# Sign of float64 weights by two integer parts on ScalarE and a second sum on GpSimd, with some softmax normalisations on VectorE

## The chip, the cores and the metric

The kernel runs on one core of a Trainium2 chip. The metric is the device time of that core in microseconds. Before the change it is 1660.12 us (median of three runs, 1659.88 to 1661.93); the execution that was profiled took 1659.89 us, of which 1658.1 us lie between its first and its last instruction. PE is TensorE, DVE is VectorE, ACT is ScalarE, POOL is GpSimd, SP is the engine that issues most DMAs.

## The reference

Attention that keeps only the 32 largest scores of each row, then a two-layer MLP with an exact GELU:

```python
# q, k, v: (8, 8, 576, 64) float32
scores = scale * np.matmul(q, k.transpose(0, 1, 3, 2))
kth = np.partition(scores, -top_k, axis=-1)[..., -top_k:-top_k + 1]   # top_k = 32
scores = np.where(scores >= kth, scores, -1000000000.0)
scores = scores - np.max(scores, axis=-1, keepdims=True)
attn = np.exp(scores)
attn = attn / (np.sum(attn, axis=-1, keepdims=True) + 1e-09)
attn_out = np.matmul(attn, v).astype(np.float32)
# (B, H, S, D) -> (4608, 512)
x = attn_out.transpose(0, 2, 1, 3).reshape(4608, 512)
h = x @ w_in                                   # w_in (512, 2048)
g = 0.5 * h * (1.0 + erf(h * inv_sqrt2))
out = (g @ w_out).astype(np.float32)           # w_out (2048, 512)
```

The two weight matrices arrive as float64, because the product of float64 random numbers with a float stays float64. The matmuls of the kernel are float32, so the kernel turns 2 x 1,048,576 doubles into floats on the chip while the first attention rows are being worked on.

## The kernel before

The program is one loop over slots `n`. A slot handles two tiles of 128 score rows of 576 columns (`e` is 0 or 1), spread over several stages of a pipeline, and up to eight pieces of the MLP. The instruction streams are laid down in this order, and each engine works through its own in order:

```python
    for n in range(ahead):
        left[0] = 7 if START < n < START + 2 * NP else 8     # START = 10, NP = 4: MLP pieces of a slot
        weights_add(unit_in(n))
        scores(n + 2)
        product = attend(n - 3)
        late = n > START
        mlp(1)
        tr = transposes(n - 2)
        # ... (cut)
        softmax(n - 1, 0)
        mlp(1)
        if not late:
            softmax(n - 1, 1)
        # ... transposes, MLP pieces (cut)
        if late:
            softmax(n - 1, 1)
        add_small(n - 1)                # den += 1e-9, on POOL
        # ... more pieces, GELUs (cut)
        top_k(n, {3: lambda: inverse(n - 1)})
        threshold(n)                    # neg, bias: two tiny POOL operations
        normalise(n - 1)

        weights_sign(unit_in(n))
        weights_size(unit_in(n + 1))
        if n >= FIRST:
            load_weights(n + 2)
```

`top_k` is 8 MAX8 and 6 MATCH_REPLACE8 on DVE per slot, with the reciprocal of the row sums of the slot before at its end. `normalise` multiplies the exponentials by that reciprocal, and the transposes of the next slot read them:

```python
    def normalise(i):
        # ... (cut)
        for e in range(2):
            s = row(i, e)                                   # 128 x 576 float32, in place
            nc.gpsimd.tensor_scalar(s, s, st["rden"][:, e : e + 1], None, op0=ALU.mult)
```

The weights come in 16 units of 128 x 1024 numbers, one to a slot: slots 1 to 15, and the last in slot 17. The DMA drops the lowest 16 bits of the first double, so that in the loaded words a 32-bit word holds bits 16 to 47 of a double (`w`) and the next 16 bits hold its sign, its 11 exponent bits and 4 mantissa bits (`first`). The magnitude of the float, read as an integer, is `(first without sign - EXP0) * 2^19 + w * 2^-13`:

```python
    def parts(u):
        t, dst = words[u], weights_of(u)[3]
        return t[:, :, 0::2], t.bitcast(u16)[:, :, 2::4], dst

    def weights_size(u):
        # ... (cut)
        w, first, dst = parts(u)
        size = stage.tile([P, 2 * WS], bf16, tag="size", name="size")
        size = size.rearrange("p (a n) -> p a n", a=first.shape[1])
        nc.scalar.activation(size, first.bitcast(bf16), func=AF.Abs)          # drops the sign bit
        nc.scalar.activation(
            dst.bitcast(i32), size.bitcast(i16), func=AF.Relu, bias=low, scale=2.0**19
        )
        if not on_pool(u):
            nc.scalar.activation(w.bitcast(i32), w.bitcast(u32), func=AF.Copy, scale=2.0**-13)

    def on_pool(u):
        return SLOT_OF[u] >= START                          # slots 10 to 15 and 17

    def weights_add(u):
        if u in words:
            w, _, dst = parts(u)
            d = dst.bitcast(i32)
            if on_pool(u):
                nc.gpsimd.tensor_scalar(
                    w.bitcast(i32), w.bitcast(u32), 2.0**-13, None, op0=ALU.mult
                )
            nc.gpsimd.tensor_tensor(d, d, w.bitcast(i32), op=ALU.add)

    def weights_sign(u):
        if u in words:
            _, first, dst = parts(u)
            top = dst.bitcast(u16)[:, :, 1::2]
            nc.vector.scalar_tensor_tensor(
                out=top, in0=first, scalar=0x8000, in1=top,
                op0=ALU.bitwise_and, op1=ALU.bitwise_or,
            )
        made.add(u)
```

So a unit costs two or three operations on ACT, one or two on POOL, and one on DVE, which copies the sign bit into the finished magnitude.

Of the kernel before, what the change touches and what calls it, by code (L numbers as in the profile page):

```python
# [14 lines left out]
def kernel(  # L15
# [19 lines left out]
    nc = tc.nc  # L35
    f32, i32, u32 = mybir.dt.float32, mybir.dt.int32, mybir.dt.uint32
    bf16, i16, u16 = mybir.dt.bfloat16, mybir.dt.int16, mybir.dt.uint16
    AF = mybir.ActivationFunctionType
    ALU = mybir.AluOpType

    B, H, S, D = q.shape
    P = 128
# [13 lines left out]
    scale = 1.0 / float(D) ** 0.5  # L56
# [3 lines left out]
    const = ctx.enter_context(tc.tile_pool(name="const", bufs=1))  # L60
# [41 lines left out]

    WS = 512
    NWI = KO // 2 * (DFF // WS)
    UNITS = NWI + FT // 2
    EXP0 = 16 * (1023 - 127)
    assert DM == WS and KO == 4 and FT == 16

    def weights_of(u):

        if u < NWI:
            c, r = u // 2 * WS, u % 2 * 2
            return w_in, r, c, w_in_sb[:, r : r + 2, c : c + WS]
        r = 2 * (u - NWI)
        return w_out, r, 0, w_out_sb[:, r : r + 2, :]
# [6 lines left out]
    words = {}  # L124
    low = const.tile([P, 1], f32, name="low")
    nc.gpsimd.memset(low, -EXP0 * 2.0**19)


    SLOT_OF = {u: FIRST + i + (i == UNITS - 1) for i, u in enumerate(ORDER)}
    UNIT_IN = {n: u for u, n in SLOT_OF.items()}  # L130
    unit_in = UNIT_IN.get

    def load_weights(n, queue=None):
# [6 lines left out]
        if src.dtype == f32:  # L140
            for x in range(2):
                queue.dma_start(
                    out=dst[:, x], in_=src[(r + x) * P : (r + x + 1) * P, c : c + WS]
                )
# [7 lines left out]
        else:  # L152
            t = stage.tile([P, 2, 2 * WS], f32, tag="words", name="words")
        for a in range(2):
# [5 lines left out]

    def parts(u):

        t, dst = words[u], weights_of(u)[3]
        return t[:, :, 0::2], t.bitcast(u16)[:, :, 2::4], dst

    def weights_size(u):
        if u not in words:
            return
        w, first, dst = parts(u)
        size = stage.tile([P, 2 * WS], bf16, tag="size", name="size")  # L170
        size = size.rearrange("p (a n) -> p a n", a=first.shape[1])
        nc.scalar.activation(size, first.bitcast(bf16), func=AF.Abs)
        nc.scalar.activation(
            dst.bitcast(i32), size.bitcast(i16), func=AF.Relu, bias=low, scale=2.0**19
        )
        if not on_pool(u):
            nc.scalar.activation(w.bitcast(i32), w.bitcast(u32), func=AF.Copy, scale=2.0**-13)

    def on_pool(u):

        return SLOT_OF[u] >= START

    def weights_add(u):
        if u in words:
            w, _, dst = parts(u)
            d = dst.bitcast(i32)
            if on_pool(u):
                nc.gpsimd.tensor_scalar(
                    w.bitcast(i32), w.bitcast(u32), 2.0**-13, None, op0=ALU.mult
                )  # L190
            nc.gpsimd.tensor_tensor(d, d, w.bitcast(i32), op=ALU.add)

    made = set()

    def weights_sign(u):
        if u in words:
            _, first, dst = parts(u)
            top = dst.bitcast(u16)[:, :, 1::2]
            nc.vector.scalar_tensor_tensor(  # L199
                out=top, in0=first, scalar=0x8000, in1=top,  # L200
                op0=ALU.bitwise_and, op1=ALU.bitwise_or,
            )
        made.add(u)


# [48 lines left out]
    def row(i, e):  # L254
        return S_of[i][:, e * S : (e + 1) * S]
# [97 lines left out]
    def inverse(i):  # L353
        if i < 0 or i >= N:
            return
        st = stat_of[i]
        nc.vector.reciprocal(st["rden"], st["den"])  # L357

    def add_small(i):
        if i < 0 or i >= N:  # L360
            return
        st = stat_of[i]
        nc.gpsimd.tensor_scalar(st["den"], st["den"], 1e-9, None, op0=ALU.add)  # L363

    def softmax(i, e):

        if i < 0 or i >= N:
            return
        st, s = stat_of[i], row(i, e)
        nc.scalar.activation(s, s, func=AF.Prelu, bias=st["neg"][:, e, 1:2], scale=1.0, alpha=STEEP)  # L370
        nc.scalar.activation(  # L371
            s, s, func=AF.Exp, bias=st["bias"][:, e : e + 1], scale=1.0,
            accum_out=st["den"][:, e : e + 1],
        )

    def normalise(i):
        if i < 0 or i >= N:
            return
        st = stat_of[i]
        for e in range(2):  # L380
            s = row(i, e)
            nc.gpsimd.tensor_scalar(s, s, st["rden"][:, e : e + 1], None, op0=ALU.mult)  # L382

    pt_now = [None]
    ptt = const.tile([P, 2, NJ, P], f32, name="ptt")
# [2 lines left out]
    def transposes(i):  # L388

        if i < 0 or i >= N:  # L390
            return []
        t, s = items[i][1], S_of.pop(i)

        def tails():
            tp = ps.tile([P, 512], f32, tag="tp", name="tp_t")
            if t < NM:
                if t % 2 == 0:
                    pt_now[0] = work.tile([P, 2 * NM + 1, 2 * P], f32, tag="pt", name="pt")
                nc.tensor.transpose(tp[:, 0:P], s[:, SM : S + TL], ident)  # L399
                nc.scalar.copy(out=pt_now[0][:, 2 * NM, t % 2 * P : (t % 2 + 1) * P], in_=tp[:, 0:P])  # L400
            else:
                pt_now[0] = ptt
                for r in range(2):
                    nc.tensor.transpose(
                        tp[0:TL, r * P : (r + 1) * P], s[:, r * S + SM : (r + 1) * S], ident
                    )
                for e in range(2):
                    c = slice(e * TL, (e + 1) * TL)
                    nc.scalar.copy(
                        out=halves(ptt[c, 0, NM, :], e, NJ * P), in_=halves(tp[0:TL, 0 : 2 * P], e, P)  # L410
                    )

        def main(e):
            tp = ps.tile([P, 512], f32, tag="tp", name="tp")
            first = e * (S + TL if t < NM else S)
            for j in range(NM):
                nc.tensor.transpose(  # L417
                    tp[:, j * P : (j + 1) * P], s[:, first + j * P : first + (j + 1) * P], ident
                )
            if t < NM:  # L420
                dst = pt_now[0][:, e * NM : (e + 1) * NM, t % 2 * P : (t % 2 + 1) * P]
            else:
                dst = ptt[:, e, 0:NM, :]
            nc.scalar.copy(out=dst, in_=tp.rearrange("p (j n) -> p j n", j=NM))  # L424

        return [tails] + [lambda e=e: main(e) for e in range(2)]
# [137 lines left out]
    def run_gelus():  # L564
        while waiting:
            gelus(waiting.pop(0))
# [9 lines left out]
    def mlp(n):  # L576
        for _ in range(n):
            if done[0] >= len(pieces) or pieces[done[0]][0] > ready[0] or left[0] == 0:
                return
            pieces[done[0]][1]()  # L580
            done[0] += 1
            left[0] -= 1
# [4 lines left out]
    stage = staging.enter_context(tc.tile_pool(name="stage", bufs=1))  # L587
# [26 lines left out]
    first = {2: (0, 1, 1), 3: (2, 2, 3)}  # L614
    prep_in = {}
    for pair in range(2, n_pairs):
        b, p = divmod(pair, NP)
# [3 lines left out]
    for n in range(ahead):  # L621

        left[0] = 7 if START < n < START + 2 * NP else 8
# [6 lines that stand above are left out]
        if product and n > START and done[0] < len(pieces) and pieces[done[0]][0] > ready[0]:  # L630

            for piece in tr[:1]:
                piece()
            tr, ready[0] = tr[1:], n_tok[0]
# [5 lines that stand above are left out]
        prep = prep_in.pop(n, [])  # L640
        if len(prep) > 1 and len(tr) == 3:
            tr, prep = tr[:1] + prep[:1] + tr[1:], prep[1:]
        for piece in tr[:-1]:
            piece()
            ready[0] = n_tok[0]
            mlp(1)
        ready[0] = n_tok[0]
        if late:
            softmax(n - 1, 1)
        add_small(n - 1)  # L650
        for piece in tr[-1:] + prep:
            piece()
            mlp(1)

        run_gelus()
        mlp(left[0])
        run_gelus()
        if n < N:
            top_k(n, {3: lambda: inverse(n - 1)})
        else:  # L660
            inverse(n - 1)
        threshold(n)
        normalise(n - 1)

        weights_sign(unit_in(n))
        weights_size(unit_in(n + 1))
        if n >= FIRST:
            load_weights(n + 2)
        if n <= NP:
            load("v", n)  # L670
# [38 lines left out]
```

## Time and profile before

| | before |
|---|---|
| time, median of 3 | 1660.12 us |
| PE busy | 1590.1 us (96%) |
| DVE busy | 1428.5 us (86%) |
| ACT busy | 1182.8 us (71%) |
| POOL busy | 661.6 us (40%) |
| the sign on DVE (line 199) | 16 operations, 1291 to 1379 ns, first at 31.6 us, last at 213.5 us |
| one normalisation on POOL (line 382) | 288 operations, median 1722 ns |

The page of a profile gives the busy time of each engine over the whole span and its share in 40 slices of 41.45 us. A view of stages gives the busy time of each engine between two moments. A timeline lists instructions in order with start and duration; "x2" merges two of a kind, and a bracket tells how long the engine had stood idle and what released it. Neighbouring DVE or ACT instructions overlap by some 0.1 us in these lists, so the cost of one in a full row is the distance from its start to the start of the next, not its duration.

### The profile page before, as it was taken

What the parts mean: (1) busy time and instruction counts of PE and PEld (TensorE: products, weight loads), DVE (VectorE), ACT (ScalarE), POOL (GpSimd) and SP (SyncE); (2) the same over time, 40 slices, a digit from 0 to 9 for tenths busy, and PEclk for the clock granted to TensorE, in tenths of its full rate; (3) what the DMA queues carried; (4) which work ended last, traced back from release to release, by engine and by line L of the source; (5) the groups of instructions that cost most, each with busy time, mean ns of one, the idle gap of its engine ahead of it and who ended that gap; (6) DMA issues with size and microseconds to landing.
All of it is one profiled execution on the core that took longest, in us unless ns stands there. A gap on an engine that the chain in (4) does not pass through costs nothing.

```text
span 1658.1 us, 25071 instructions
## 1 busy us (share of the span) xinstructions
PE 1590.1 (96%) x8832; PEld 1079.1 (65%) x8832; DVE 1428.5 (86%) x3043; ACT 1182.8 (71%) x2131; POOL 661.6 (40%) x761
## 2 busy tenths in 40 slices
PE   6559999999999999999999999999999999999999
PEld 4336566766666667676666667676666666666665
DVE  7999899998999898998999888998889898999800
ACT  6888777777777777777777777777777777777720
POOL 3769653333333333333333333333333333333300
PEclk7779999999999999999999999999999999999999
DMA  6422210011100111001110111001110001000000
GB/s 162 138 99 97 84 49 1 14 29 29 37 14 22 29 30 35 1 28 36 29 28 1 43 29 43 1 14 28 44 35 1 27 15 32 5 14 3 5 13 13
DMA packets 126621, 56.14 MB, mean 34 GB/s; under 512 B 117760, under 2 KB 117792, under 8 KB 126496
## 3 DMA queue, kind: packets, MB, share of 16 engines
q1 hardware_dynamic: 125376, 54.25, 12.2%
q8 instruction: 70, 1.15, 0.3%
q14 instruction: 55, 0.45, 0.1%
q10 hardware_dynamic: 1056, 0.26, 0.1%
q0 software_dynamic: 64, 0.03, 0.0%
HBM read 45.08 MB, written 9.44 MB: 33 GB/s over the span
## 4 chain that ended last, share of the span: by engine, by line
PE 89%; DVE 6%; ACT 2%; POOL 1%; issue 1%; POOLq 0%; ACTq 0%
PE h_ps L500 30%; PE y_ps L536 29%; PE o L448 8%; PE s_ps L284 7%; PE tp L417 7%; DVE top L331 3%; DVE rest L334 3%; PE tp_qk L239 2%; PE t_ps L280 2%; PE o L459 1%; PE tp_t L399 1%; PE s_ps L305 1%; POOL s L382 1%; DVE w_in_sb L199 0%; ACT s L371 0%
## 5 line engine op out<-in xcount | busy, mean ns | idle before, releaser
L331 DVE MAX8 top<-rest 128x8 f32<-128x576 f32 x864 | 609.9, 748 | 0.0
L500 PE MATMUL h_ps<-xT,w_in_sb 128*128 128x256 f32 (+1 forms) x2560 | 554.5, 361 | 3.7 <-ACT g L511 3.7
L536 PE MATMUL y_ps<-w_out_sb,g 128*128 128x512 f32 x1152 | 549.4, 599 | 0.0
L382 POOL TENSOR_SCALAR s<-s,rden 128x576 f32<-128x576 f32 x288 | 493.5, 1723 | 1.0 <-issue 0.7
L500 PEld LDWEIGHTS h_ps<-xT,w_in_sb 128*128 128x128 f32 x2560 | 429.2, 191 | 66.7 <-issue 16.8
L334 DVE MATCH_REPLACE8 rest<-top,rest 128x576 f32<-128x576 f32 x576 | 423.7, 744 | 0.0
L363 POOL TENSOR_SCALAR den<-den 128x2 f32<-128x2 f32 x144 | 32.0, 222 | 831.7 <-ACT s L371 830.7
L536 PEld LDWEIGHTS y_ps<-w_out_sb,g 128*128 128x128 f32 x1152 | 195.0, 190 | 166.4 <-issue 164.3
L288 ACT ACTIVATE s<-s_ps 128x1024 f32<-128x1024 f32 x128 | 131.5, 1027 | 166.5 <-PE s_ps L284 144.8
L371 ACT ACTIVATE s<-s,bias 128x576 f32<-128x576 f32 x288 | 223.3, 775 | 13.0 <-ACT s L370 0.4
L370 ACT ACTIVATE s<-s,neg 128x576 f32<-128x576 f32 x288 | 224.0, 778 | 0.5 <-POOL neg L346 0.4
L424 ACT COPY pt<-tp 128x512 f32<-128x512 f32 x256 | 147.1, 575 | 103.6 <-PE tp L417 103.4
L334 DVE MATCH_REPLACE8 rest<-top,s 128x576 f32<-128x576 f32 x288 | 211.9, 744 | 0.0
L417 PEld LDWEIGHTS tp<-ident,s 128*128 128x128 f32 x1152 | 147.9, 145 | 89.3 <-issue 59.2
L331 DVE MAX8 top<-s 128x8 f32<-128x576 f32 x288 | 201.9, 743 | 3.9 <-ACT s L289 3.9
L417 PE MATMUL tp<-ident,s 128*128 128x128 f32 x1152 | 177.9, 279 | 4.3 <-ACT pt L400 4.2
L448 PE MATMUL o<-pt,raw_v 128*64 128x256 f32 x1280 | 155.1, 389 | 0.0
L284 PE MATMUL s_ps<-qk 64*128 64x256 f32 x1024 | 151.8, 417 | 0.7 <-ACT s L288 0.7
L357 DVE RECIPROCAL rden<-den 128x2 f32<-128x2 f32 x144 | 23.2, 161 | 139.9 <-POOL den L363 139.3
L448 PEld LDWEIGHTS o<-pt,raw_v 128*64 128x64 f32 x1280 | 87.5, 139 | 65.8 <-issue 23.9
L284 PEld LDWEIGHTS s_ps<-qk 64*128 64x128 f32 x1024 | 91.8, 194 | 23.7 <-issue 1.8
L511 ACT ACTIVATE g<-h_ps 128x512 f32<-128x512 f32 x144 | 78.6, 595 | 34.0 <-PE h_ps L500 33.2
(63 smaller groups left out, 1070.2 us busy)
## 6 DMA issues: line engine op xcount, KB each, us to landing
raw_q<-in_q_dram SPq DMA_DIRECT2D x64, 128.0 KB, 2.3
raw_v<-in_v_dram SPq DMA_DIRECT2D x64, 128.0 KB, 2.4
out_dram<-y SPq DMA_DIRECT2D x32, 256.0 KB, 2.1
w_out_sb<-in_moe_w_in_dram SPq DMA_DIRECT2D x16, 511.8 KB, 4.8
raw_k<-in_k_dram SPq DMA_DIRECT2D x62, 128.0 KB, 2.4
w_out_sb<-in_moe_w_out_dram SPq DMA_DIRECT2D x10, 511.8 KB, 3.9
words<-in_moe_w_out_dram SPq DMA_DIRECT2D x6, 511.8 KB, 4.7
raw_q<-in_q_dram SPq DMA_DIRECT2D x64, 16.0 KB, 2.2
```

Of the source, the lines that this page charges most:

```text
L284: nc.tensor.matmul(s_ps[:, e, c * 256 : (c + 1) * 256], lhsT=lhsT[rows, :], rhs=qk[rows, KT + c * 256 : KT + (c + 1) * 256], start=True, s ...
L288: nc.scalar.activation(spread(s, S + TL, SM), s_ps, func=AF.Copy, scale=scale)
L331: nc.vector.max(st["top"][:, e, 8 * r : 8 * r + 8], cur[e])
L334: nc.vector.match_replace(rest[:, e], st["top"][:, e, 8 * r : 8 * r + 8], cur[e], LOWEST)
L370: nc.scalar.activation(s, s, func=AF.Prelu, bias=st["neg"][:, e, 1:2], scale=1.0, alpha=STEEP)
L371: nc.scalar.activation(s, s, func=AF.Exp, bias=st["bias"][:, e : e + 1], scale=1.0, accum_out=st["den"][:, e : e + 1],)
L382: nc.gpsimd.tensor_scalar(s, s, st["rden"][:, e : e + 1], None, op0=ALU.mult)
L417: nc.tensor.transpose(tp[:, j * P : (j + 1) * P], s[:, first + j * P : first + (j + 1) * P], ident)
L424: nc.scalar.copy(out=dst, in_=tp.rearrange("p (j n) -> p j n", j=NM))
L448: nc.tensor.matmul(o[e * D : (e + 1) * D, 0:n], lhsT=vt[:, j, e, :], rhs=pt[:, e * NM + j if j < NM else 2 * NM, :], start=(j == 0), stop= ...
L500: nc.tensor.matmul(h_tile(u)[:, i, :], lhsT=w_in_sb[:, ko, f * P : (f + 1) * P], rhs=xT[:, ko, c0 : c0 + n], start=(ko == 0), stop=(ko == ...
L536: nc.tensor.matmul(y_of[sub], lhsT=g_of[u][:, i, sub * P : (sub + 1) * P], rhs=w_out_sb[:, f, :], start=(f == 0), stop=(f == FT - 1),)
```

## The change

The sign no longer comes from DVE. ACT makes two whole-number parts from `first` read as a signed 16-bit number: a Relu gives the part of positive numbers and zero for negative ones, as before; a Prelu gives the part of negative numbers, sign bit and all, and a number that rounds to zero for positive ones (scale 2^-21 and slope 2^40 below zero together give 2^19). The second part overwrites the word that held `first`. POOL adds both parts and `w`. The step that took the absolute value is gone, so ACT still has two such operations per unit; POOL has one sum more, and DVE none. To relieve POOL, the normalisation of the slot is moved to DVE: one of the two tiles where the next slot has a unit whose multiplication is done on ACT, both where that multiplication is on POOL too. All other slots keep both on POOL.

```diff
+    high = const.tile([P, 1], f32, name="high")
+    nc.gpsimd.memset(high, EXP0 * 2.0**-21)
...
     def parts(u):
-        t, dst = words[u], weights_of(u)[3]
-        return t[:, :, 0::2], t.bitcast(u16)[:, :, 2::4], dst
+        t, dst = words[u], weights_of(u)[3].bitcast(i32)
+        return t[:, :, 0::2], t.bitcast(mybir.dt.int16)[:, :, 2::4], t[:, :, 1::2].bitcast(i32), dst
...
-        w, first, dst = parts(u)
-        size = stage.tile([P, 2 * WS], bf16, tag="size", name="size")
-        size = size.rearrange("p (a n) -> p a n", a=first.shape[1])
-        nc.scalar.activation(size, first.bitcast(bf16), func=AF.Abs)
-        nc.scalar.activation(
-            dst.bitcast(i32), size.bitcast(i16), func=AF.Relu, bias=low, scale=2.0**19
-        )
+        w, first, below, d = parts(u)
+        nc.scalar.activation(d, first, func=AF.Relu, bias=low, scale=2.0**19)
+
+        nc.scalar.activation(below, first, func=AF.Prelu, bias=high, scale=2.0**-21, alpha=2.0**40)
...
     def weights_add(u):
         if u in words:
-            w, _, dst = parts(u)
-            d = dst.bitcast(i32)
+            w, _, below, d = parts(u)
             if on_pool(u):
                 nc.gpsimd.tensor_scalar(
                     w.bitcast(i32), w.bitcast(u32), 2.0**-13, None, op0=ALU.mult
                 )
+            nc.gpsimd.tensor_tensor(d, d, below, op=ALU.add)
             nc.gpsimd.tensor_tensor(d, d, w.bitcast(i32), op=ALU.add)
-
-    def weights_sign(u):
-        # ... (the whole function, as above)
...
-    def normalise(i):
+    def normalise(i, on_dve):
...
-            nc.gpsimd.tensor_scalar(s, s, st["rden"][:, e : e + 1], None, op0=ALU.mult)
+            (nc.vector if e >= 2 - on_dve else nc.gpsimd).tensor_scalar(
+                s, s, st["rden"][:, e : e + 1], None, op0=ALU.mult
+            )
...
-        normalise(n - 1)
-
-        weights_sign(unit_in(n))
+        u = unit_in(n + 1)
+
+        normalise(n - 1, 0 if u not in words else 2 if on_pool(u) else 1)
+
         weights_size(unit_in(n + 1))
```

## The prediction

> **What bounds the kernel now.** I read the page first (engines over the 40 slices), then the kernel in stages, then the timelines of DVE, POOL and ACT in one slot, then the waits.
>
> The 40 slices:
>
> ```profile
> PE   6559999999999999999999999999999999999999
> DVE  7999899998999898998999888998889898999800
> POOL 3769653333333333333333333333333333333300
> ```
>
> The first four slices differ from the rest: PE half idle, DVE full, POOL at its busiest. All weight units are made there (first sign at 31.6 us, last at 213.5). The stages (columns: stretch, its length, then busy time of each engine, granted clock, DMA):
>
> ```profile
> 12.00:32.85 20.85, 11.72 (x58) 7.46 (x58) 20.66 (x43) 16.68 (x27) 4.24 (x5) 0.74 0.63 164
> 32.85:119.98 87.13, 47.47 (x236) 32.34 (x238) 87.13 (x176) 72.60 (x121) 59.48 (x49) 0.68 0.38 117
> 119.98:224.74 104.76, 93.42 (x517) 62.53 (x514) 96.88 (x198) 82.03 (x141) 80.53 (x60) 0.98 0.28 84
> 224.74:1440.00 1215.26, 1215.26 (x6958) 828.41 (x6958) 1100.15 (x2363) 896.03 (x1640) 457.71 (x564) 1.00 0.10 25
> ```
>
> In 32.85 to 119.98 us (slots 2 to 9) DVE is busy for all 87.13 us: it alone sets the pace, 10.9 us a slot, and PE waits at half load. From 119.98 to 224.74 us (slots 10 to 18) the MLP has begun and nothing is full: DVE 96.9, PE 93.4, ACT 82.0, POOL 80.5 of 104.8 us. After that PE has no gap for 1215 us. So whatever the first 225 us lose or gain goes straight to the end, and nothing after them can be changed by this edit, which keeps PE's program as it is.
>
> The end of slot 4 on DVE, and POOL beside it:
>
> ```profile
> 62.88 1.42 DVE L331 MAX8 top<-rest 128x8 f32<-128x576 f32 x2
> 64.20 0.15 DVE L357 RECIPROCAL rden<-den 128x2 f32<-128x2 f32 x1
> 64.27 1.30 DVE L199 SCALAR_TENSOR_TENSOR w_in_sb<-w_out_sb,w_in_sb 128x1024 uint16<-128x1024 uint16 x1
> 65.45 1.42 DVE L331 MAX8 top<-s 128x8 f32<-128x576 f32 x2
> ...
> 64.38 1.25 POOL L346 TENSOR_SCALAR neg<-top 128x4 f32<-128x4 f32 x1 [2.86 <-DVE rden L357]
> 65.71 0.19 POOL L349 TENSOR_TENSOR bias<-neg 128x2 f32<-128x2 f32 x1
> 65.89 3.43 POOL L382 TENSOR_SCALAR s<-s,rden 128x576 f32<-128x576 f32 x2
> 69.28 2.40 POOL L191 TENSOR_TENSOR w_out_sb<-w_out_sb 128x1024 int32<-128x1024 int32 x1
> 71.77 0.22 POOL L363 TENSOR_SCALAR den<-den 128x2 f32<-128x2 f32 x1
> ```
>
> The reader is to see three things. The sign costs DVE 65.45 - 64.27 = 1.18 us from start to start (1.22 in other slots). POOL's tiny neg takes 1.25 us here, as long as the sign lasts; at 129.80 us, where it does not start behind a sign, it takes 0.23. And POOL has time: 2.86 us idle before neg.
>
> Who waits in the stage from 120 us:
>
> ```profile
> PE tp_t L404 <- POOL s L382: 2.9, 2, 1.5
> PE tp_t L399 <- POOL s L382: 2.8, 3, 1.7
> PE h_ps L500 <- ACT g L511: 2.6, 1, 2.6
> DVE rden L357 <- POOL den L363: 7.6, 5, 4.3
> ```
>
> 5.7 us of PE's idle time there end with POOL's normalisation. DVE's 7.6 us end with den, which in turn waits for ACT's exponentials (21.0 us in the same view): those are PE's and ACT's lateness, not POOL's.
>
> **What the Trainium skill says.** "VectorE: DVE Perf Modes", section "Mode 2×_2P — use both read ports for one tensor": a float32 tensor_scalar from SBUF to SBUF makes two elements a cycle. Section "The TRN2 errata — SBUF-src ops pay a fixed extra latency per instruction" gives 58 cycles plus the elements by the mode, at 0.96 GHz. The trace agrees for one element a cycle: MAX8 of 576 would be 634 cycles, 0.66 us, and two of them take 1.32 from start to start (62.88 to 64.20). No run shows the two-element mode yet. "SBUF — State Buffer", section "Who interferes with whom": a DVE operation with two SBUF inputs or in a two-port mode and a GpSimd operation hold a shared port in turn. The neg of 1.25 against 0.23 us agrees. "ScalarE: Activation LUTs", section "What ACT_TABLE_LOAD costs": the cost does not depend on the function. The trace agrees: Relu 1.15, Abs 1.14, Copy 1.13 us for 1024 elements.
>
> **The change part by part.**
>
> *DVE, slots 1 to 9.* Removed: 9 signs x 1.21 = 10.9 us, all on the path. Added: an estimate for a normalisation of 576 elements at two a cycle is (58 + 288) / 0.96 = 0.36 us. It needs the reciprocal just before it, so it must wait for that one's end: 0.15 - 0.07 us of it remain, and some 0.05 for the signal; I take 0.15. Slots 1 to 8 get one normalisation (8 x 0.51 = 4.1), slot 9 two (0.87): 5.0 us. Port: neg wants to start at the same moment as the normalisation; one of them waits for the other. If it is DVE half the time, 9 x 0.5 x 0.2 = 0.9 us. Sum: -10.9 + 5.0 + 0.9 = -5.0 us.
>
> *ACT.* Abs and Relu (62.58 to 64.81 us, 2.23) become Relu and Prelu, 2 x 1.05 start to start without a wait between: -0.1 us per unit. No table load is added: Prelu already runs in this kernel on either side of a GELU without one. ACT has about 9.2 us of work per early slot (72.6 us in eight slots), below the 10.3 us that a slot is to take. No gain, no new bound.
>
> *POOL, slots 1 to 9.* Plus 2.40 for the second sum, minus 1.72 for one normalisation, and neg is held up for 0.4 instead of 1.2. About the same load, 7.4 of 10.3 us; it stays off the path.
>
> *POOL, slots 10 to 17.* The row there now: multiplication 2.99, sum 2.41, normalisations 3.42, neg, bias and den 1.5 to 1.7, about 10.0 us of a slot. After: 2.99 + 4.8 + 0.9, 8.7 us. So it is relieved.
>
> *DVE in slots 10 to 17.* Seven signs x 1.22 = 8.5 us go, six pairs of normalisations x 0.87 = 5.2 come (slots 10 to 14 and 16): 96.9 falls to 93.6 us.
>
> *PE in the same stage.* Three waits for POOL's normalisation (1.66, 0.58 and 0.52 us) follow slots in which both tiles move to DVE, where they end some 1 us after the reciprocal and not 4.6. They should vanish: -2.8 us. The two before the transposes of slot 18 (1.54 and 1.41) stay on POOL, but bias there takes 1.11 us behind a sign and should take 0.19: -0.9 us. With DVE's shorter row that is about -4 us; the wait for the GELU (2.57) and the table loads stay.
>
> Sum: -5 - 4 = -9, so 1660 becomes 1651.
>
> **The rivals.**
>
> *A: DVE takes the gain back.* The normalisation does not reach two elements a cycle, or waits for a whole POOL operation. At one element a cycle it is 0.66 us: 9 slots cost 0.3 more each, 10 x 0.3 = 3 us of the first stage, and 3.6 in the second. If it waited 1.7 us for POOL's own normalisation each time, the slot would be longer than before, 8 x 0.5 to 1 us. Against the latter: in POOL's order neg, bias and its own normalisation come after the same reciprocal, so DVE should be first. A would make 1655 to 1664.
>
> *B: POOL's longer chain becomes the bound in slots 10 to 15.* Both sums now follow ACT's two parts, and den, which comes after them in POOL's order, frees the reciprocal. In slot 11 ACT ends its part at 135.2 us, so POOL would end at 135.2 + 2.99 + 4.8 = 143.0 if the multiplication too had to wait for ACT (they touch the same tile), 140.0 if not; den ran at 141.57. That is up to 1.5 us in each of two or three slots. For it: den already stood within 0.1 us of the reciprocal in slot 10. Against it: three of POOL's 10 us are gone. B would take back 2 to 4 us: 1653 to 1655.
>
> *C: slots 10 to 18 were DVE's more than I think.* Then the whole slack of 104.8 - 93.6 us opens up, or most of it: another -4, 1646 to 1647. Against it: DVE waits 7.6 us there itself.
>
> **Range and chances.** The middle is 1651.5, a little above the sum for B. The range takes A in its mild form at one end and most of C at the other: 1645.5 to 1657.5. 2% is 33 us; the stage in which anything can happen is 225 us long and its removable part under 25, so faster by 2% has 0.01, slower by 2% 0.01.
>
> **What the profile after would show.** The first step is right if DVE is still full in slots 2 to 9 and a slot takes 10.1 to 10.5 us, with a normalisation of about 0.45 us in the list; it is wrong if such a normalisation lasts 0.7 us or more. The waits of the transposes (line 399) for a normalisation should vanish around slots 10 to 15. B shows as DVE's reciprocal waiting for den with POOL's sums right before it. The stage of 1215 us should have the same length. The prediction fails if ACT sets the pace of the early slots, or if an early slot is longer than 10.9 us.

## The result, and the profile after

| | before | after |
|---|---|---|
| time, median of 6 | 1660.12 us | 1655.54 us (1654.10 to 1656.98) |
| ratio | | 0.9967, 95% interval 0.9954 to 0.998 |
| profiled span | 1658.1 us | 1653.7 us |

The change makes the kernel 0.3% faster: 4.6 us by these medians, inside the predicted range, but only half of the predicted 8.6. The size of the gain depends on which runs are compared: all 44 runs of the kernel before in this study have a median of 1661.9 us, the ten of the changed kernel 1655.4, which makes 6.5 us, and the trace of before is of one of its shorter runs (1659.89 us). The 40 slices of the kernel after:

```profile
PE   6669999999999999999999999999999999999999
DVE  7999899989999889998989988998889898999800
POOL 3677543333333333333333333333333333333300
```

On DVE the slices hardly differ; POOL's fullest slice has gone from 9 to 7. The stages of the kernel after, cut at the same slots as before (stretch, length, busy PE, weight loads, DVE, ACT, POOL, clock, DMA):

```profile
33.62:115.89 82.27, 50.54 (x234) 32.23 (x236) 81.70 (x178) 73.05 (x121) 57.63 (x49) 0.62 0.42 132
115.89:220.49 104.60, 93.24 (x518) 62.67 (x517) 93.93 (x203) 83.47 (x143) 69.25 (x51) 0.98 0.25 76
220.49:1435.75 1215.26, 1215.26 (x6958) 828.86 (x6958) 1100.02 (x2362) 896.13 (x1640) 457.52 (x563) 1.00 0.10 25
```

Slots 2 to 9 went from 87.13 to 82.27 us, with DVE still full. Slots 10 to 18 went from 104.76 to 104.60, although POOL lost 11 us of work there and DVE 3. In the long stage PE is busy without a gap, as before; that it takes as long as before is read from the last column of the table below, since the stretch here was cut to the length of the one before.

The same end of slot 4 on DVE, and POOL beside it, in the kernel after:

```profile
63.19 0.14 DVE L349 RECIPROCAL rden<-den 128x2 f32<-128x2 f32 x1
63.36 0.52 DVE L375 TENSOR_SCALAR s<-s,rden 128x576 f32<-128x576 f32 x1
63.81 1.41 DVE L323 MAX8 top<-s 128x8 f32<-128x576 f32 x2
...
63.35 0.23 POOL L338 TENSOR_SCALAR neg<-top 128x4 f32<-128x4 f32 x1 [2.58 <-DVE rden L349]
63.66 0.28 POOL L341 TENSOR_TENSOR bias<-neg 128x2 f32<-128x2 f32 x1
63.92 1.73 POOL L375 TENSOR_SCALAR s<-s,rden 128x576 f32<-128x576 f32 x1
65.62 2.40 POOL L193 TENSOR_TENSOR w_out_sb<-w_out_sb 128x1024 int32<-128x1024 int32 x1
68.10 2.40 POOL L194 TENSOR_TENSOR w_out_sb<-w_out_sb 128x1024 int32<-128x1024 int32 x1
70.58 0.22 POOL L355 TENSOR_SCALAR den<-den 128x2 f32<-128x2 f32 x1
```

One normalisation costs DVE 63.81 - 63.36 = 0.45 us, and 0.17 from the reciprocal's start to its own. Neg is back at 0.23 us, only bias shows a trace of the shared port (0.28 against 0.19).

Who kept PE waiting in slots 10 to 18 of the kernel after, and DVE in the same stretch. The "tails" are the last 64 columns of both tiles of a slot, which PE transposes first (`tp_t`) and ACT copies to `pt`; `tp` are the transposes of the other columns, `h_ps` is the first MLP product, `g` its GELU:

```profile
PE tp L412 <- ACT pt L395: 3.8, 3, 1.5
PE tp_t L399 <- POOL s L375: 3.0, 2, 1.6
PE h_ps L495 <- ACT g L506: 2.7, 1, 2.7
...
DVE rden L349 <- POOL den L355: 10.0, 6, 4.0
```

The same wait for the copy of the tails in the kernel before:

```profile
PE tp L417 <- ACT pt L400: 2.0, 2, 1.3
```

The waits of line 399 of before, which should vanish (2.8 us), are gone: that line is 394 here, and no wait of it is left. Line 399 here is line 404 of before, the two transposes of slot 18, whose 2.9 us are now 3.0. In place of the vanished waits PE waits longer for ACT's copy of the tails (3.8 us, it was 2.0) and 0.6 us for another of ACT's copies, and DVE waits 10.0 us for den and not 7.6. Most of the time was moved, not saved.

For the experiments below, one measure is used throughout: the distances between the reciprocals on DVE, which stand at the end of every slot. The table gives them for one trace of each kernel (two where it says so), in us; the last column is from the end of slot 18 to the end of the kernel.

| kernel | slots 2 to 9 | slot 10 | slots 11 to 17 | slot 18 | rest |
|---|---|---|---|---|---|
| before | 87.23 | 11.03 | 83.68 | 11.23 | 1433.5 |
| after | 82.37 | 10.77 | 84.24 | 10.43 | 1433.5 |
| after, a second trace | 82.38 | 10.78 | 86.24 | 10.44 | 1433.5 |
| normalisations alone moved | 91.91 | 12.90 | 90.98 | 12.41 | 1434.9 |
| conversion alone | 78.67 | 12.42 | 90.47 | 10.62 | 1434.8 |
| one of two late ones on DVE | 82.38 | 10.93 | 83.42 | 10.31 | 1433.5 |
| early ones on POOL | 78.64 | 12.48 | 87.09 | 10.70 | 1434.8 |
| no Prelu in late units | 82.37 | 10.77 | 80.10 | 10.43 | 1433.5 |
| no second sum | 82.38 | 10.77 | 86.06 | 10.42 | 1433.5 |
| tails first, two traces | 82.37, 82.39 | 10.78, 10.77 | 81.22, 83.50 | 10.43, 10.43 | 1433.5, 1433.5 |
| PE kept busy | 92.56 | 10.93 | 87.94 | 10.46 | 1435.1 |
| PE kept busy, tails first | 93.38 | 10.96 | 85.47 | 10.43 | 1433.5 |
| the same, early ones on POOL | 92.55 | 10.95 | 85.48 | 10.43 | 1433.5 |

### The profile page after: what moved, and what is told of

Its sections match the earlier page's. It is cut to its first block, busy times and chain, and to the rows that moved or that the text cites. A ratio compares the mean times of both kernels' runs of the same rounds, so it can differ in the third digit from the quotient of the medians.

```text
span 1653.7 us, 25056 instructions
## 1 busy us (share of the span) xinstructions
PE 1593.8 (96%) x8832; PEld 1080.5 (65%) x8832; DVE 1419.6 (86%) x3049; ACT 1184.1 (72%) x2131; POOL 650.5 (39%) x756
## 3 DMA queue, kind: packets, MB, share of 16 engines
q1 hardware_dynamic: 125376, 54.25, 12.2%
q8 instruction: 70, 1.15, 0.3%
## 4 chain that ended last, share of the span: by engine, by line
PE 92%; ACT 6%; DVE 1%; issue 1%; POOL 0%; ACTq 0%; POOLq 0%; DVEq 0%
PE h_ps L495 30%; PE y_ps L531 30%; PE o L443 9%; PE s_ps L276 8%; PE tp L412 8%; PE tp_qk L231 2%; PE t_ps L272 2%; ACT s L363 1%; PE o L454 1%; ACT s L362 1%; PE s_ps L297 1%; PE tp_t L394 1%; ACT s L280 1%; POOL s L375 0%; PE warm L595 0%
## 5 line engine op out<-in xcount | busy, mean ns | idle before, releaser
L375 POOL TENSOR_SCALAR s<-s,rden 128x576 f32<-128x576 f32 x266 | 456.0, 1723 | 0.8 <-issue 0.4
```

What stands on the lines that cost most here:

```text
L375: (nc.vector if e >= 2 - on_dve else nc.gpsimd).tensor_scalar(s, s, st["rden"][:, e : e + 1], None, op0=ALU.mult)
```

## The experiments

The theory after the first traces: slots 2 to 9 are DVE's row and gave what was predicted; slots 10 to 18 are set by PE and ACT in their fixed orders, so an earlier normalisation only waits elsewhere. Rivals: POOL's second sum took the gain back there (rival B), or the second tile's move was worth something that another loss hides.

**The changed kernel again.** No edit.

> The changed kernel once more, beside the others of this group. 1654 to 1657 us. If the 0.9 us by which its first row of scores came later in the first trace belongs to the change, it is there again; if it is the warm-up matmuls' clock, the start differs from run to run in kernels whose start is the same.

1654.93 us (1654.37 to 1656.68), ratio 0.9961 (0.9946 to 0.9975). Its first scores came 0.1 us later than in the kernel before, and not 0.9: the 16 warm-up matmuls ahead of them (32 entries of the trace) lasted 5.77 us in the trace of before, 6.67 in the first of after and 5.87 here. So 0.9 us of the first trace is chance, and not the change's. The gain of slots 2 to 9 is the same to 0.01 us; slots 11 to 17 differ by 2 us between the two traces.

**The normalisations alone.** The conversion of before, with the new line in the slot:

```diff
-        normalise(n - 1)
+        u = unit_in(n + 1)
+        normalise(n - 1, 0 if u not in words else 2 if on_pool(u) else 1)
```

> The old conversion with the sign on DVE, and only the normalisations moved. If the first stage is DVE's row alone, a slot there takes 10.9 + 0.6 = 11.5 us, eight of them 5 us more than before. If moved normalisations bring nothing in slots 10 to 18 (theory: PE and ACT in their fixed order set the pace there), the whole is 1664 to 1667 us. If they are worth the 3 to 4 us of PE's waits for them that I predicted (rival), it is 1660 to 1663.

1676.26 us, ratio 1.0088 (1.0073 to 1.0103): some 10 us above the theory's guess and more above the rival's. Slots 2 to 9 are as expected (8 x 11.5 = 92). Slots 10 to 14 take 12.9 us each, and DVE is full in them: its search for the 32 largest (9.7 us, as in the early slots of the run below with every normalisation on POOL), 1.1 for the reciprocal and both normalisations, and 2.1 for the sign from start to start. DVE and POOL at the end of slot 12 of this kernel show why the sign takes so long:

```profile
162.46 0.95 DVE L382 TENSOR_SCALAR s<-s,rden 128x576 f32<-128x576 f32 x2
163.32 2.27 DVE L199 SCALAR_TENSOR_TENSOR w_in_sb<-w_out_sb,w_in_sb 128x1024 uint16<-128x1024 uint16 x1
...
162.68 0.35 POOL L349 TENSOR_TENSOR bias<-neg 128x2 f32<-128x2 f32 x1
163.11 3.12 POOL L188 TENSOR_SCALAR words<-words 128x1024 int32<-128x1024 uint32 x1
```

POOL, free of its normalisations, starts its multiplication 0.2 us ahead of the sign, and the sign takes 2.27 us where it took 1.32; so it is in six slots (2.19 to 2.31 us). Before, the sign always started first, and it was POOL's neg or bias that was lengthened. "SBUF — State Buffer" of the Trainium skill, section "Who interferes with whom", says just that: issue order decides who blocks. Here the later one did not wait for the whole of the earlier one (3.12 us) but lost 0.95. That is 6 us of the some 10. The theory had also left out that DVE's row alone is longer in these slots: 9.7 + 1.1 + 1.2 = 12.0 us even with an undisturbed sign, where slot 10 of before took 11.0. So the two halves of the change do not add up: one is 14 us slower alone, and the pair is faster than the kernel before.

**The conversion alone.**

```diff
-        normalise(n - 1, 0 if u not in words else 2 if on_pool(u) else 1)
+        normalise(n - 1, 0)
```

> The new conversion, and every normalisation on POOL as before. If DVE alone set the pace of the first stage, a slot there would fall to 9.7 us, 4 us less than in the changed kernel, and the whole would be 1651. But POOL then has 3.4 + 4.8 + 1.2 us a slot, and ACT 9.4 to 10.2: with them as the next bound (theory) a slot stays at 10.1 to 10.4. In slots 10 to 15 POOL has 12.3 us a slot (3.0 + 4.8 + 3.4 + 1.1) and must become the bound: 5 to 8 us lost there. Theory: 1660 to 1664 us.

1660.73 us, ratio 0.9995 (0.9986 to 1.0004): no difference from before, as the theory had it. Slots 2 to 9 take 78.67 us, 3.7 less than with one normalisation on DVE; that is faster than expected of POOL and ACT. In slots 12 to 14 POOL is the bound (in slot 11 it waits 2.3 us for ACT's second part besides). Its row in slot 12, with 12.3 us from den (138.19) to den, and DVE's wait between 108 and 225 us:

```profile
138.98 3.43 POOL L375 TENSOR_SCALAR s<-s,rden 128x576 f32<-128x576 f32 x2
142.50 2.99 POOL L190 TENSOR_SCALAR w_out_sb<-w_out_sb 128x1024 int32<-128x1024 uint32 x1
145.57 2.40 POOL L193 TENSOR_TENSOR w_in_sb<-w_in_sb,w_out_sb 128x1024 int32<-128x1024 int32 x1
148.05 2.40 POOL L194 TENSOR_TENSOR w_in_sb<-w_in_sb,w_out_sb 128x1024 int32<-128x1024 int32 x1
150.53 0.22 POOL L355 TENSOR_SCALAR den<-den 128x2 f32<-128x2 f32 x1
...
DVE rden L349 <- POOL den L355: 25.3, 9, 5.9
```

So relieving POOL in the late units is needed, to pay for the second sum. It is no gain by itself, as the run before this one shows.

**One of two late normalisations back on POOL.**

```diff
-        normalise(n - 1, 0 if u not in words else 2 if on_pool(u) else 1)
+        normalise(n - 1, 0 if u not in words else 1)
```

> In slots 9 to 14 and 16 only one of the two normalisations is on DVE, the other on POOL. POOL's row in those slots is 3.0 + 4.8 + 1.7 + 0.9 = 10.4 us of some 11.6. Theory (PE and ACT set the pace there, moved normalisations bring nothing by themselves): within 1 us of the changed kernel, 1654 to 1657. Rival (the normalisation's lateness costs what I predicted): 1.5 to 2 us slower or more.

1655.10 us, ratio 0.9961 (0.9946 to 0.9975), the same as the changed kernel beside it. The second tile's move brings nothing; the rival falls.

**Both early normalisations back on POOL.**

```diff
-        normalise(n - 1, 0 if u not in words else 2 if on_pool(u) else 1)
+        normalise(n - 1, 0 if u not in words else 2 if on_pool(u) else 0)
```

> Slots 1 to 8 keep both normalisations on POOL (as in the run with all of them on POOL, whose slots there took 9.7 to 9.9 us against 10.3), slots 9 to 14 and 16 have both on DVE (as in the changed kernel). If the two stages add up (theory: the first is DVE's row, and POOL's 9.6 us a slot fits just beside it), 3.7 us less than the changed kernel: 1651 to 1652. Rival: ACT, which had 10.2 us of every 10.3 in slots 5 to 9, comes late into slot 10 and gives the gain back there: 1653 to 1655.

1656.28 us, ratio 0.9968 (0.9956 to 0.998): nothing won. DVE is 3.7 us ahead at the end of slot 9 and has lost it by the end of slot 11 (12.48 us for slot 10, 15.72 for slot 11). ACT's part of the unit of slot 10, in the changed kernel and then in this one:

```profile
112.13 1.24 ACT L174 ACTIVATE w_out_sb<-w_out_sb,low 128x1024 int32<-128x1024 int16 x1
```

```profile
112.15 1.24 ACT L174 ACTIVATE w_out_sb<-w_out_sb,low 128x1024 int32<-128x1024 int16 x1
```

In both it stands at the same time: ACT did not follow DVE's gain. From slot 5 on these operations stand 9.9 us apart in this kernel (62.85 to 112.15 us), of which ACT works 9.1 and waits the rest for PE; the 10.2 of the expectation is too high, in the changed kernel ACT works 9.0 us a slot there. ACT begins its next unit 6.67 us after the reciprocal of slot 10 here and 2.98 us after it in the first trace of the changed kernel, and slot 11 is longer by the same 3.7 us. So the mechanism of the rival is the right one, though the median lies a little above the rival's range.

**Less work on ACT in the late units.** This kernel leaves out the negative part of the seven units of slots 10 to 15 and 17; POOL adds w twice.

```diff
-        nc.scalar.activation(below, first, func=AF.Prelu, ...)
+        if not on_pool(u):
+            nc.scalar.activation(below, first, func=AF.Prelu, ...)
...
-            nc.gpsimd.tensor_tensor(d, d, below, op=ALU.add)
+            nc.gpsimd.tensor_tensor(d, d, w.bitcast(i32) if on_pool(u) else below, op=ALU.add)
```

> Leaves out the second part (Prelu) of the seven units of slots 10 to 15 and 17; POOL adds w a second time in its place, so its row stays. Negative weights of these units come out as nonsense. ACT loses 7 x 1.15 = 8 us between 112 and 201 us. If ACT's fixed order sets the pace of slots 10 to 18 together with PE (theory): 2 to 4 us faster than the changed kernel, 1651 to 1653. If it is PE's row alone or DVE's: no change, 1654 to 1656.

1651.79 us, ratio 0.9946 (0.993 to 0.9963): 3 to 4 us below the changed kernel by the medians, with intervals that overlap (0.9954 to 0.998 and 0.9946 to 0.9975 there). Its trace is of its shortest run (1650.67 us). Slots 11 to 17 take 80.1 us in it, 4 to 6 less than in the two traces of the changed kernel; without slot 11, in which two traces of one kernel differ by 2 us, slots 12 to 17 take 69.3 us against 72.2 and 72.0. So of the 8 us taken from ACT somewhat less than half comes through. PE's longest waits between 114 and 220 us there:

```profile
PE tp_t L400 <- POOL s L376: 3.0, 2, 1.6
PE h_ps L496 <- ACT g L507: 2.7, 1, 2.7
PE tp L413 <- ACT pt L396: 2.5, 2, 1.4
```

The wait for the copy of the tails falls from 3.8 to 2.5 us.

**Less work on POOL.** This kernel leaves out the sum of the second part in all units.

```diff
-            nc.gpsimd.tensor_tensor(d, d, below, op=ALU.add)
```

> Leaves out POOL's sum of the second part in all 16 units (negative weights come out without their magnitude and sign part), ACT unchanged. POOL loses 2.4 us a slot. Theory (POOL is beside the path in all slots): 1654 to 1656. Rival B of the prediction (the chain from ACT's parts over two sums to den holds up DVE): 2 to 4 us faster.

1655.96 us, ratio 0.9967 (0.9954 to 0.998): the same as the changed kernel, though 38 us of POOL's work (16 x 2.4) are gone. Rival B falls.

**The tails ahead of the softmax.** If ACT's order is what holds PE's transposes, moving the copy forward must help. In the branches in front of the first softmax half, for slots 10 to 18:

```diff
+        elif START <= n <= START + 2 * NP:
+            for piece in tr[:1]:
+                piece()
+            tr = tr[1:]
         softmax(n - 1, 0)
```

> In slots 10 to 18 the transpose of the tails and its copy on ACT stand ahead of the first softmax half, not behind it, since the normalised rows are now there earlier. Theory: PE's waits for that copy (3.8 us in slots 10 to 18 of the changed kernel) go, and 2 to 3 us of the whole, 1652 to 1653. Rival: the softmax, and den behind it, only come later by as much, and nothing is won: 1654 to 1656.

1654.36 us (1651.77 to 1654.71), ratio 0.9953 (0.9938 to 0.9968): a median in the rival's range. Once more:

> The kernel with the tails ahead of the softmax in slots 10 to 18 once more, in more rounds. Its first trace had slot 10 to slot 18 in 91.7 us (94.7 and 96.7 in two traces of the changed kernel), but its median was only 0.6 to 1.2 us below the changed kernel's. Theory: 1 to 3 us faster than the changed kernel's 1655, 1652 to 1654. Rival: no difference, 1654 to 1656.

1652.85 us (1652.03 to 1654.02), ratio 0.9947 (0.9935 to 0.996). PE's longest waits between 114 and 220 us in the second trace:

```profile
PE h_ps L495 <- ACT g L506: 3.4, 1, 3.4
PE tp_qk L231 <- ACT pt L419: 2.8, 4, 1.0
PE tp_t L399 <- POOL s L375: 1.6, 2, 1.4
```

The wait for the tails' copy has gone from the list. Slots 13 to 15 take 10.8 to 10.9 us each, where the changed kernel has 11.7, 12.2 and 14.9; slot 16 then takes 15.8, where it has 11.8, so the long slot is mostly put off by one. In the table slots 11 to 17 are 0.7 to 5 us shorter, by which traces are compared; slots 12 to 17 alone take 69.9 us in both traces, 2.1 to 2.3 less than in the two of the changed kernel. This is the fastest complete kernel of the study: its nine runs have a median of 1653.4 us, 2.0 below the ten of the changed one. The two intervals of the ratios (0.9935 to 0.996 and 0.9954 to 0.998) touch, so the size of that gain is not certain.

**PE kept busy in slots 2 to 9.** The traces of one kernel differed by 2 us in slot 11, and PE's granted clock reached its full value at different times. Two stretches of the first and second trace of the changed kernel (the clock is the third number from the end):

```profile
116.00:118.00 2.00, 2.00 (x18) 1.15 (x15) 2.00 (x6) 0.20 (x2) 2.00 (x1) 0.94 0.32 131
```

```profile
116.00:118.00 2.00, 2.00 (x12) 1.21 (x12) 2.00 (x6) 1.19 (x2) 1.96 (x1) 0.51 0.00 0
```

Slot 11 took 12.0 us in the first and 14.3 in the second. In the two traces with the tails first it took 11.3 and 13.6, with 1.00 and 0.50 as the clock of this stretch. To see whether the clock is the cause, 24 and 12 matmuls of the identity were put where PE waits:

```diff
+        t = ps.tile([P, 512], f32, tag="l1", name="warm")
+        for _ in range(count):          # 24 ahead of the transposes, 12 before the last of them
+            nc.tensor.matmul(t[:, 0:P], lhsT=ident, rhs=ident, start=True, stop=True)
```

> The changed kernel with 36 matmuls of the identity in each of slots 2 to 9, in two places where PE waits; their result is not used. In the changed kernel PE's clock is at half there, and full only from 115 to 119 us on, so that slot 10's products take 3.1 to 3.4 us and not 2.3, and the copies of ACT wait for slow transposes. Theory (that clock is part of what made slot 10 late and two traces of one kernel differ): slot 10 starts PE at full clock, 1 to 2 us gained, 1653 to 1654, and a narrower range of runs. Rival: the added matmuls hold up PE's own row in the early slots, and ACT behind it, 1656 or more.

> Both of the former together. If the two gains are apart: 1651 to 1653. If the clock is not the cause: as the tails alone.

> Both of the former, and the normalisations of slots 1 to 8 on POOL. With these on POOL alone DVE came to the end of slot 9 3.6 us earlier, but ACT's part of slot 9 ended at the same time as in the changed kernel (112.15 against 112.13 us) and nothing was won. Theory (ACT's row sets the pace from slot 5 on): ACT's work is the same here, only its waits for PE are shorter (2.7 us between 81 and 112 us); at most 2 us below the one with the former two, 1650 to 1652. If POOL's row (9.6 us a slot) holds it up: as the former two or slower.

The theories of all three missed, and the rival of the first was right: 1669.56, 1666.51 and 1666.62 us, ratios 1.0045 (1.0031 to 1.0059), 1.0026 (1.0016 to 1.0037) and 1.0028 (1.0017 to 1.004). PE in one early slot of the first:

```profile
70.39 5.62 PE L620 MATMUL warm<-ident 128*128 128x128 f32 x48
75.86 0.27 PE L394 MATMUL tp_t<-ident,s 128*128 128x128 f32 x1
75.96 0.60 PE L412 MATMUL tp<-ident,s 128*128 128x128 f32 x4
76.40 2.84 PE L620 MATMUL warm<-ident 128*128 128x128 f32 x24
79.08 0.60 PE L412 MATMUL tp<-ident,s 128*128 128x128 f32 x4
```

A float32 matmul of the program is two entries of the trace, so the added work was 8.4 us a slot and not half of it: it filled PE and held up ACT behind it (slots 2 to 9: 92.6 us). The clock was full there, but the run cannot tell what that was worth.

The traces lead further back, to slot 4. PE's product with v there (20 matmuls), in the first and the second trace of the changed kernel:

```profile
54.14 2.68 PE L443 MATMUL o<-pt,raw_v 128*64 128x256 f32 x20
53.34 3.94 PE L443 MATMUL o<-pt,raw_v 128*64 128x256 f32 x20
```

The clock between 52 and 56 us was 0.65 in the first and 0.50 in the second. ACT waits 1.07 and 2.33 us for this product and does not make the loss good in the slots that follow, in which it works some 9 of every 10.3 us. It begins its next unit 2.98 and 5.24 us after the reciprocal of slot 10, and slot 11 takes 12.02 and 14.28 us: both differ by 2.26. Seven traces of the changed kernel and its late variants agree: where this product took 2.7 to 2.9 us slot 11 took 10.8 to 12.0, where it took 3.9 to 4.2 slot 11 took 13.6 to 14.3. So slot 11 shows ACT's lateness, which begins with a slow product at a low clock seven slots earlier. This is read from traces; no run changed that clock alone.

## Why the prediction was right in range, and which half of it failed

- **DVE, slots 1 to 9: right.** Predicted -5.0 us; measured 87.23 + 11.03 to 82.37 + 10.77, which is -5.1. By its terms: a normalisation was put at 0.36 us and is 0.45; the wait for the reciprocal was put at 0.15, and reciprocal and normalisation together take 0.62 from start to start, 0.55 more than the reciprocal's own 0.07 (I had 0.51). The port wait that I added for caution, 0.9 us in all, did not come, so the two errors cancel: that the sum is right to 0.1 us is luck, that DVE alone sets this stage is not. The early slot of 10.27 to 10.35 us lies in the range that was named.
- **ACT: wrong in sign, small.** Predicted -0.1 us per unit (and 9.2 us of work a slot, where 72.6 / 8 is 9.1). The unit of slot 5 in the kernel after:

```profile
61.84 1.23 ACT L174 ACTIVATE w_out_sb<-w_out_sb,low 128x1024 int32<-128x1024 int16 x1
63.10 1.23 ACT L176 ACTIVATE w_out_sb<-w_out_sb,high 128x1024 int32<-128x1024 int16 x1
64.23 1.12 ACT L178 ACTIVATE w_out_sb<-w_out_sb 128x1024 int32<-128x1024 uint32 x1
65.25 1.00 ACT L280 ACTIVATE s<-s_ps 128x1024 f32<-128x1024 f32 x1
```

  65.25 - 61.84 = 3.41 us against 3.27 before (62.58 to 65.85). Each part takes 1.23 and not 1.15 us, and the second still waits for the first, whose input it overwrites. "No new bound" was only just true: the run with the early normalisations on POOL shows that ACT did not follow when DVE's slot fell to 9.8 us.
- **POOL: right.** 57.6 us in the eight slots, 7.2 each (7.4 predicted), and 3.12 + 2.40 + 2.41 + 0.80 = 8.7 us in slot 10, as predicted.
- **DVE in slots 10 to 18: right.** 93.9 us busy (93.6 predicted). It bought nothing.
- **PE in slots 10 to 18: this step failed.** I wrote that the three waits for POOL's normalisation "should vanish: -2.8 us", and with DVE's shorter row made it -4. They did vanish, but slots 11 to 17 took 0.6 to 2.6 us more than in the trace of before, and slots 10 to 18 together went from 105.9 us to 105.4 and 107.5. If the 6.5 us between the medians of all runs hold, some 1.4 are left for these slots beside the 5.1 of the first stage; that is an estimate, and the traces do not show where they would lie. Taking a wait away where it is seen is worth its length only if what comes next on PE is ready. Here it was not: PE's transposes share two PSUM buffers (tag `tp` in the kernel), the second group of `tp` needs the one that held the tails, and ACT frees it by copying them only after the first softmax half, in its own order. Leaving 8 us of work out on ACT made the kernel 3 to 4 us faster, leaving 38 us out on POOL changed nothing, and moving that copy forward removed that wait and took 2.1 to 2.3 us from slots 12 to 17. The -0.9 us ahead of slot 18's transposes did not come either. Bias fell from 1.11 to 0.19 us as predicted, but the two waits stayed (1.64 and 1.41 us, from 1.54 and 1.41), because the reciprocal came 1.59 us after the start of PE's product in front of these transposes (209.76 and 208.17 us) and not 0.69 (213.43 and 212.74): slot 17 on DVE now holds two normalisations and takes 10.79 us, where it had no sign and took 9.90. That slot 18 fell from 11.23 to 10.43 us is the other side of this, DVE's sign that is gone from it; slots 17 and 18 together take 21.1 us before and 21.2 after.
- **Rivals.** A (DVE takes it back) and B (POOL's chain) are refuted by the 0.45 us and by the run without the second sum. C did not happen. The rival that was true, ACT's order, I had only among the things that would break the first stage.

## What to carry to other kernels

In a stage where no engine is full, do not add up the waits that name the engine you relieve: follow the waiting engine one step further, to the buffer or the row that it needs next, and see whether that is ready. A change that moves work between two engines that share a port has to be judged as a whole, because it also changes which of them starts first: half of this one cost 14 us alone. And leaving work out on one engine at a time, even if the output is then useless, tells in one run which row sets the pace.

## What the runs showed of the hardware that was not expected

- A DVE operation with two inputs (the sign) took 1.32 us when it started before POOL's work and 2.27 us when POOL's multiplication had started 0.2 us earlier; POOL's 3.12 us was little more than its 2.98 without.
- A float32 normalisation of 128 x 576 in place costs 0.45 us on DVE and 1.72 on POOL.
- Reading 16-bit numbers 8 bytes apart and writing 32-bit integers costs ACT 1.23 us for 1024. A dense 16-bit input with the same output took 1.15, and the spaced input with a 16-bit output 1.14.
- The granted TensorE clock differed between traces of one kernel: 0.94 and 0.51 between 116 and 118 us, 0.65 and 0.50 between 52 and 56 us, where a product of 20 matmuls took 2.68 and 3.94 us. The 16 warm-up matmuls at the start took 5.8 to 6.7 us. Differences of 1 to 2 us between traces of one kernel begin at these places.
